# Gate and val of groups 2 to 5 by seven half-size block products instead of eight

## The chip, the cores and the metric

The kernel runs on one core of a Trainium2 chip. The metric is device time in microseconds (us), the median of several runs. In the text PE is TensorE (matmuls; its weight loads are PEld), DVE is VectorE, ACT is ScalarE, POOL is GpSimd, SP is SyncE, which issues most DMAs.

## The reference

Retention attention over 4 batches, 8 heads, 768 positions, 64 channels a head, then RMS norm and a SwiGLU layer over 3072 tokens (512 channels, 1536 hidden):

```python
intra = np.einsum('bhic,bhjc->bhij', qb, kb) * Dmask[None]
intra = np.einsum('bhij,bhjd->bhid', intra, vb)
inter = np.einsum('bhid,bhde->bhie', qb * lam_pow[None], kv_state)
out[:, :, sl] = intra + inter
kv_state = lam_block * kv_state + np.einsum('bhsd,bhse->bhde', kb_dec, vb)
...
xn = x / rms * rms_g
g = xn @ w_gate
silu = g * (1.0 / (1.0 + np.exp(-g)))
val = xn @ w_val
return (silu * val @ w_out).astype(np.float32)
```

All in float32.

## The kernel before, in words

The 3072 tokens make six groups of 512 (m = 0 to 5), the 1536 hidden channels twelve blocks of 128 (f = 0 to 11). A *unit* is one block of one group, written 2.4 for group 2, block 4. The units run in this order: group 0 blocks 0 to 5, all of group 1, group 0 blocks 6 to 11, then groups 2, 3, 4, 5 whole. In the code `u` counts them, so unit 2.0 is u = 24, and the parity of u is that of f there.

To keep float32's precision a matrix is stored as two float16 parts, high and low, and a product is three matmuls: high x high, low x high, high x low. Gate and val of a unit each contract 512 channels in four steps of 128, so each is 12 matmuls of 128x128 weights and 512 tokens into one PSUM bank: gate into `pg`, val into `pv` (function `product`, line 699). Then ACT makes the Silu of `pg` (`sg`, line 784), DVE multiplies with `pv` (`mul`, line 791), ACT casts the high part (`high`, line 801), DVE subtracts the low one (`low`, line 808). One unit later PE multiplies these with `wo`: four out blocks (`out`, t = 0 to 3) of three matmuls each, lines 718 to 720, which add up in four banks `acc` over the twelve units and leave at f = 11.

Between these stands the attention of a later group, one *pair* of heads at a time (class `Pair`): `scores` into `pa` (the two-bank tile of the pool ps_att), `decay_k` (ACT) and `decay_q` (POOL) in place on the loaded `qkv`, `decay_a` (DVE), `state_sums` into `pst`, `states` (DVE), `mix_chunks` and `mix_states` into `po`, then `keep_output` and `keep_squares` (ACT) and `add_squares` (POOL or DVE). `load_next` issues the next DMA.

When a group's four pairs are done, class `Norm` makes its normalized operand: `split_squares` (ACT, POOL), `row_sums` (two matmuls), `seed` and three times `refine` on DVE (each three dependent instructions of 512), then `parts`: for each of four channel blocks `scaled` (DVE), `high` (ACT cast) and `low` (DVE). `halve_o(f)` rewrites `wo` of one block as float16 parts: two instructions on ACT, one on DVE, one add on POOL; the table `HALVE` says in which u.

The order of the work is written by hand: within `tc.manual_schedule` each engine's instructions stand in the order of the code, and the tile framework adds the semaphores. PSUM has eight banks: four `acc`, `pg`, `pv`, and the tile of two in ps_att. Several tags of SBUF buffers are shared: `raw_o` (2 buffers), `in` (4), `w` (1), `t` (3).

Of the kernel before, what the change touches and what calls it, by code (L numbers as in the profile page):

```python
# [9 lines left out]
F32 = mybir.dt.float32  # L10
# [7 lines left out]
P = 128  # L18
# [5 lines left out]
def retention_swiglu_kernel(  # L24
# [146 lines left out]
    WS = 2.0**15  # L171
# [84 lines left out]
    def halve_o(f):  # L256
# [11 lines left out]
        nc.gpsimd.tensor_add(t[:, 1], rest[:, 0], rest[:, 1])  # L268

# [89 lines left out]
    class Weights:  # L359
# [56 lines left out]
        def scale(self, c=slice(0, 2)):  # L416

            if c.start == 0:
# [7 lines left out]
                self.sc[:, c].bitcast(I32), self.e2[:, c], -1.0, float(205 * EXP),  # L426
# [36 lines left out]
    class Pair:  # L463
# [143 lines left out]
    class Norm:  # L607
# [79 lines left out]
        def parts(self):  # L687
            for kk in range(NK):
                self.scaled(kk)
                self.high(kk)  # L690
                if kk:
                    self.low(kk - 1)
            self.low(NK - 1)
# [66 lines left out]

    class Hidden:
# [19 lines left out]

        def silu(self):
            self.sg = tmp.tile([P, G], F32, tag="t", name=f"sg_{self.m}_{self.f}")
            nc.scalar.activation(self.sg, self.pg, AF.Silu, scale=cg[:, self.f, 0:1])  # L784
# [10 lines left out]
        def high(self):  # L795
            if self.half:
                both = hp.tile([P, 2, G], F16, tag="hh", name=f"hh_{self.m}_{self.f}")
# [378 lines left out]
    def unit(u, h, before, late, ready, wt, new, done, norm, step):  # L1176
# [33 lines left out]
        for f in HALVE.get(u, []):  # L1210
            halve_o(f)
        if new and done:
            done.mix()
            done.keep()
# [5 lines left out]
        elif norm:  # L1220
            norm.parts()
# [19 lines left out]
    HALVE = {18: [6, 7], 19: [8, 9], 20: [10, 11], 23: [0, 1], 24: [2, 3], 25: [4, 5]}  # L1241

    with tc.manual_schedule(
# [7 lines left out]
        for u, (m, f) in enumerate(units):  # L1251
# [5 lines left out]
            nxt = max(2, u // NF + 1)  # L1257
            step = u - (nxt * NF - (8 if nxt == 2 else 11))
            new = Pair(nxt, step) if nxt < NG and 0 <= step < NP else None
            done = last if nxt < NG and 1 <= step <= NP else None  # L1260
            if nxt < NG and step == NP + 1:
                norm = Norm(nxt)
                norm.split_squares()
            wt = Weights(TAKE[u]) if u in TAKE else None
            unit(u, h, before, late, ready, wt, new, done, norm, step)
            late, ready = None if wt else ready, wt
            if step == NP + 2:
                norm = None
            before, last = h, new
        before.out()  # L1270
# [72 lines left out]
```

## Time and profile before

| what | value |
|---|---|
| median of 3 runs | 674.52 us (674.17 to 674.59) |
| span of the profiled execution | 673.0 us |
| matmuls on PE | 4143, busy 666.7 us |
| mean granted TensorE clock | 1.000 |
| 128x512 gate matmuls, line 699 | 864 of 379 ns, begun one each 0.216 us |
| the same for val | 864 |
| out matmuls, lines 718 to 720, float16 | 3 x 216 |

In the rows that follow, a group's row reads: line, engine, operation, output<-inputs by the program's names, partitions x elements, count, then busy us and mean ns of one, then the engine's idle time just before these and what ended it. A timeline row reads: start in us, length in us, engine, line, operation, and in brackets the idle time before with its releaser. A row of the waits reads: who waited, for whom, us in all, times, longest. A matmul's own length (379 ns) includes its way through the array; the next begins after 0.216 us.

### The profile page before, as it was taken

Reading aid. Unit: us, or ns where it says so; the run is one execution under the profiler, and the core shown is the slowest. Engines: PE = TensorE matmul, PEld = TensorE weight load, DVE = VectorE, ACT = ScalarE, POOL = GpSimd, SP = SyncE. Lnnn points to the kernel's source line nnn. Section 1 sums busy time; section 2 is a strip of 40 time slices with the busy share of each in tenths; the row PEclk is TensorE's granted clock in tenths of the full one; section 3 lists DMA queues with packets and bytes.
Section 4 is the critical chain, followed back from the end, with each engine's and each line's share of the span. In section 5 each row is a group of like instructions: output and inputs, shape, how many; then the busy total and the mean of one; then the engine's idle time right before and its main releaser. Section 6 shows DMA issues by size and latency. Waiting matters only on the chain.

```text
span 673.0 us, 9893 instructions
## 1 busy us (share of the span) xinstructions
PE 666.7 (99%) x4143; PEld 356.6 (53%) x4143; DVE 322.9 (48%) x575; ACT 248.2 (37%) x438; POOL 78.9 (12%) x76
## 2 busy tenths in 40 slices
PE   9999999999999999999999999999999999999997
PEld 8746665555565444554444555444455444444443
DVE  6798857787464486323712322732332462211112
ACT  3786556676325345222212222221331221211111
POOL 2301030011215203220000111000021000000000
PEclk9999999999999999999999999999999999999999
DMA  8975603441015101131001123000100000100001
GB/s 316 366 245 197 247 7 122 161 156 63 1 64 188 63 0 64 64 126 63 1 0 63 48 79 99 27 0 1 63 1 1 1 0 1 63 0 1 0 1 62
DMA packets 14299, 50.96 MB, mean 76 GB/s; under 512 B 1712, under 2 KB 1968, under 8 KB 12848
## 3 DMA queue, kind: packets, MB, share of 16 engines
q1 hardware_dynamic: 13968, 49.69, 20.5%
q8 instruction: 32, 0.52, 0.3%
q10 hardware_dynamic: 288, 0.66, 0.3%
q14 instruction: 11, 0.09, 0.0%
HBM read 44.05 MB, written 6.29 MB: 75 GB/s over the span
## 4 chain that ended last, share of the span: by engine, by line
PE 97%; DVE 1%; DMA 1%; issue 0%; ACT 0%; DVEq 0%
PE pg L699 28%; PE pv L699 28%; PE acc L718 10%; PE acc L720 9%; PE acc L719 9%; PE pa L478 4%; PE po L538 3%; PE po L549 3%; PE pst L507 2%; PE pss L602 1%; DMA qkv<-in_qkv_dram 1%; DVE xn L677 0%; PE pss L649 0%; DVE w L234 0%; PE unread L146 0%
## 5 line engine op out<-in xcount | busy, mean ns | idle before, releaser
L699 PE MATMUL pg<-x,wg 128*128 128x512 f16 x864 | 200.0, 379 | 0.3 <-ACT x L682 0.3
L699 PE MATMUL pv<-x,wv 128*128 128x512 f16 x864 | 199.0, 379 | 0.0
L791 DVE SCALAR_TENSOR_TENSOR sg<-pv,cv,sg 128x512 f32<-128x512 f32 x54 | 40.5, 750 | 241.7 <-PE pv L699 241.7
L699 PEld LDWEIGHTS <-wv 128*128 128x128 f16 x864 | 83.9, 98 | 101.4 <-issue 1.1
L699 PEld LDWEIGHTS <-wg 128*128 128x128 f16 x864 | 82.5, 98 | 101.4 <-issue 5.0
L720 PE MATMUL acc<-wo,hh 128*128 128x512 f16 (+1 forms) x288 | 110.3, 383 | 0.0
L719 PE MATMUL acc<-wo,hh 128*128 128x512 f16 (+1 forms) x288 | 110.2, 383 | 0.0
L784 ACT ACTIVATE sg<-pg,cg 128x512 f32<-128x512 f32 x72 | 49.3, 685 | 164.7 <-PE pg L699 164.6
L801 ACT CAST hh<-sg 128x512 f16<-128x512 f32 (+1 forms) x72 | 44.5, 618 | 162.0 <-DVE sg L791 158.2
L718 PE MATMUL acc<-wo,hh 128*128 128x512 f16 x216 | 82.0, 380 | 0.0
L498 POOL TENSOR_TENSOR qkv<-qkv,pw 128x512 f32<-128x512 f32 x22 | 28.2, 1284 | 237.6 <-PE pa L478 237.6
L808 DVE TENSOR_TENSOR hh<-sg,hh 128x512 f16<-128x512 f32 x54 | 38.0, 703 | 27.4 <-ACT hh L801 27.4
L718 PEld LDWEIGHTS <-hh 128*128 128x128 f16 x216 | 21.1, 98 | 26.6 <-issue 2.8
L720 PEld LDWEIGHTS <-hh 128*128 128x128 f16 x216 | 21.1, 98 | 25.5
L719 PEld LDWEIGHTS <-hh 128*128 128x128 f16 x216 | 21.2, 98 | 23.4
L494 DVE TENSOR_TENSOR a<-pa,mask 128x1024 f32<-128x1024 f32 x24 | 29.4, 1224 | 6.3 <-PE pa L478 6.2
L718 PE MATMUL acc<-wo,hl 128*128 128x512 f32 x72 | 32.3, 449 | 0.0
L478 PE MATMUL pa<-qkv 64*128 64x128 f32 x384 | 28.8, 291 | 0.1
L478 PEld LDWEIGHTS pa<-qkv 64*128 64x128 f32 x384 | 24.1, 193 | 8.4 <-issue 6.7
L538 PE MATMUL po<-a,qkv 128*64 128x128 f32 x384 | 25.6, 275 | 0.0
L488 ACT ACTIVATE qkv<-qkv,mask 128x256 f32<-128x256 f32 x48 | 21.7, 502 | 8.5 <-DMA qkv<-in_qkv_dram 5.1
L569 ACT COPY x<-po 128x512 f32<-128x512 f32 x22 | 12.8, 581 | 28.6 <-PE po L549 28.6
(131 smaller groups left out, 592.9 us busy)
## 6 DMA issues: line engine op xcount, KB each, us to landing
qkv<-in_qkv_dram SPq DMA_DIRECT2D x47, 512.0 KB, 4.8
raw_gv<-in_weights_dram SPq DMA_DIRECT2D x11, 1024.0 KB, 5.4
raw_o<-in_weights_dram SPq DMA_DIRECT2D x12, 512.0 KB, 3.9
out_dram<-o SPq DMA_DIRECT2D x23, 256.0 KB, 2.3
partial<-in_weights_dram SPq DMA_DIRECT2D x2, 512.0 KB, 12.4
qkv<-in_qkv_dram ACTq DMA_DIRECT2D x1, 512.0 KB, 4.2
out_dram<-o SPq DMA_DIRECT2D x1, 128.0 KB, 2.1
out_dram<-o ACTq DMA_DIRECT2D x1, 128.0 KB, 2.0
```

The source lines that it names most:

```text
L478: nc.tensor.matmul(self.pa[:, j, c, :], self.kT[r, c, :], self.qT[r, c, :], start=True, stop=True,)
L494: nc.vector.tensor_mul(self.a, self.pa, decay.broadcast_to([P, 2, GC, P]))
L498: eng.tensor_mul(self.qT, self.qT, pw[:, p : p + 1, :].broadcast_to([P, GC, P]))
L538: nc.tensor.matmul(po[r, c, :], self.v[:, c, r], self.a[:, j, c, :], start=c == 0, stop=False, skip_group_check=True,)
L699: nc.tensor.matmul(ps, w[:, kk, :], x[:, kk, :], start=i == kk == 0, stop=i == 2 and kk == NK - 1,)
L718: nc.tensor.matmul(acc, hl[:, ts_], oh, start=first, stop=False)
L719: nc.tensor.matmul(acc, hh[:, ts_], ol, start=False, stop=False)
L720: nc.tensor.matmul(acc, hh[:, ts_], oh, start=False, stop=last)
L784: nc.scalar.activation(self.sg, self.pg, AF.Silu, scale=cg[:, self.f, 0:1])
L791: nc.vector.scalar_tensor_tensor(out, self.pv, factor, self.sg, ALU.mult, ALU.mult)
L801: nc.scalar.copy(self.hh, self.sg)
L808: nc.vector.tensor_sub(self.hl, self.sg, hh)
```

## The change

For groups 2 to 5 gate and val are computed together as a product of 2x2 blocks: rows val and gate, inner index the two channel halves of 256, columns the two token halves of 256 (`HG`). Strassen's scheme in Winograd's form takes seven block products. A product is 6 matmuls of 128x128 weights and 256 tokens (three part products, two channel steps). The unit has 42 matmuls of 256 columns in place of 24 of 512.

- `weight_sums(f)` makes four sums of the weight blocks, once for each f: POOL adds high and low into `r` (two adds of 512), DVE makes four sums of 256, ACT casts the high parts (512, 256, 256), POOL subtracts the low parts. For f = 0 to 5 it follows units 0.6 to 0.11; for f = 6 to 11 (`LATE`) units 2.2 to 2.7. In `HALVE` blocks 0 to 5 are halved in units 0.9 to 0.11, formerly in 0.11 to 2.1.
- `Norm.parts` is made in two calls, and makes three sums of operand blocks more in each (`sums` on DVE, `high_sums` on ACT, `low_sums` on POOL, 768 wide). They lie in two tiles `tx`, which take two of the four `in` buffers; so `load_next` skips two calls for group 2.
- A unit (`unit_of_sums`) has two banks a and b: in even units `pg` and `pv`, in odd units the two halves of the ps_att tile (`pp`). The products go in the order 1 (a), 2 (b), 6 (a), 5 (b, anew), 7 (a), 4 (a), 3 (b). ACT copies a away after products 1, 6 and 7 (`keep`); DVE adds bank b to such a copy (`sum`) after products 2, 7 and 3. Silu is made in two halves, `mul_sums` reads SBUF alone.
- The out blocks come two units later instead of one. Pairs of the next group stand in units f = 0 to 7, one pair per two units: scores in the even, states and mixing in the odd. The norm stands in f = 8 (row sums, seed, one refinement), 9 (two refinements), 10 and 11 (parts).
- The weights' exponent constants change with the head room that the sums need.

```diff
-    WS = 2.0**15
+    WS = 2.0**13
...
-            load_next()
+            if self.m > 2 or self.p < 2:
+                load_next()
...
+        def sums(self, i):
+            a, b = self.xns[i], self.xns[2 + i]
+            a1, a2, b1, b2 = a[:, :HG], a[:, HG:], b[:, :HG], b[:, HG:]
+            t = stage.tile([P, 3, HG], F32, tag="raw_o", name=f"xt_{self.m}_{i}", bufs=2)
+            self.xt = t
+            nc.vector.tensor_sub(t[:, 0], a2, a1)
+            nc.vector.tensor_sub(t[:, 2], b2, a2)
+            nc.vector.tensor_sub(t[:, 1], b2, t[:, 0])
+            nc.vector.tensor_sub(a2, b1, t[:, 1])
+        def high_sums(self, i):
+            nc.scalar.copy(tx[SLOT_OF[self.m]][:, 0, i], self.xt)
+        def low_sums(self, i, eng=nc.gpsimd):
+            t = tx[SLOT_OF[self.m]]
+            eng.tensor_sub(t[:, 1, i], self.xt, t[:, 0, i])
+        def parts(self, i, engs):
+            self.scaled(i)
+            self.scaled(2 + i)
+            self.sums(i)
+            self.high(i)
+            self.high(2 + i)
+            self.high_sums(i)
+            self.low(i, engs[0])
+            self.low(2 + i, engs[1])
+            self.low_sums(i, engs[2])
...
+    def weight_sums(f, rest):
+        r = cvt.tile([P, 2, G], F32, tag="w", name=f"r_{f}")
+        for i, w in enumerate((wv, wg)):
+            nc.gpsimd.tensor_add(r[:, i], w[:, f, 0], w[:, f, 1])
+        v0, v1, g0, g1 = (r[:, i, j * HG : (j + 1) * HG] for i in range(2) for j in range(2))
+        t = stage.tile([P, 4, HG], F32, tag="raw_o", name=f"ws_{f}", bufs=2)
+        nc.vector.tensor_add(t[:, 0], g0, g1)
+        nc.vector.tensor_sub(t[:, 2], v0, g0)
+        nc.vector.tensor_sub(t[:, 1], g1, t[:, 2])
+        nc.vector.tensor_sub(t[:, 3], v1, t[:, 1])
...
+        nc.scalar.copy(s12[:, 0], t[:, :2])
+        nc.scalar.copy(s3[:, 0], t[:, 2])
+        nc.scalar.copy(s4[:, 0], t[:, 3])
+        nc.gpsimd.tensor_sub(s12[:, 1], t[:, :2], s12[:, 0])
+        nc.gpsimd.tensor_sub(s3[:, 1], t[:, 2], s3[:, 0])
+        nc.gpsimd.tensor_sub(s4[:, 1], t[:, 3], s4[:, 0])
...
+        def add(self, n, ps, first):
+            w, x = self.pairs[n - 1]
+            for i, (ow, ox) in enumerate(((0, 0), (1, 0), (0, 1))):
+                for k in range(2):
+                    nc.tensor.matmul(
+                        ps, w(ow, k), x(ox, k), start=first and i == k == 0,
+                        stop=i == 2 and k == 1, skip_group_check=True,
+                    )
...
+        def banks(self, u):
+            m, f = self.m, self.f
+            if u % 2:
+                t = ps_att.tile([P, 2, G], F32, tag="ps", name=f"pp_{m}_{f}")
+                self.pa, self.pb = t[:, 0, :HG], t[:, 1, :HG]
+            else:
+                self.pa = ps_gv.tile([P, G], F32, tag="pg", name=f"pa_{m}_{f}")[:, :HG]
+                self.pb = ps_gv.tile([P, G], F32, tag="pv", name=f"pb_{m}_{f}")[:, :HG]
...
+        def keep(self, i):
+            nc.scalar.copy(self.kept[:, i], self.pa)
+        def sum(self, out, i):
+            nc.vector.tensor_add(out, self.pb, self.kept[:, i])
...
-    HALVE = {18: [6, 7], 19: [8, 9], 20: [10, 11], 23: [0, 1], 24: [2, 3], 25: [4, 5]}
+    HALVE = {18: [6, 7], 19: [8, 9], 20: [10, 11], 21: [0, 1], 22: [2, 3], 23: [4, 5]}
+    def unit_of_sums(u, h, prev, outs, new, done, norm, step):
...
+        h.add(1, a, True)
+        h.add(2, b, True)
+        h.keep(0)
+        if prev:
+            prev.high()
+        h.sum(h.val[:, left], 0)
+        if prev:
+            prev.low()
...
+        if norm and step == 10:
+            norm.parts(0, (nc.gpsimd, nc.gpsimd, nc.gpsimd))
+        if norm and step == 11:
+            norm.parts(1, (nc.vector, nc.vector, nc.gpsimd))
+        h.add(4, a)
+        h.silu_half(0, a)
...
+        h.add(3, b)
+        h.sum(h.val[:, right], 1)
+        h.mul_sums()
+        if u in LATE:
+            weight_sums(LATE[u], None)
+    LATE = {26 + i: HALF + i for i in range(HALF)}
```

What that does to the order of instructions shows at three places. The first is ACT from unit 0.10 to unit 0.11. Before, between the two Silus (`sg`) stand the cast of the hidden part `hh` and the four casts of the norm (`x`):

```order
L784 ACTIVATE sg_10_2417<-pg_10_2404,cg 128x512
L801 CAST hh_10_2433<-sg_10_2417 128x512
L682 CAST x_1992<-xn_0_2436 128x512
L682 CAST x_1992<-xn_1_2439 128x512
L682 CAST x_1992<-xn_2_2443 128x512
L682 CAST x_1992<-xn_3_2447 128x512
L784 ACTIVATE sg_11_2477<-pg_11_2464,cg 128x512
```

The same place on ACT after the change; `wo` and `rest` are the halving, `tx` the sums of operand blocks, and the casts from `ws` those of the weight sums:

```order
L933 CAST hh_10_2497<-sg_10_2481 128x512
L263 ACTIVATE wo_2_2500<-wo_755,ts 128x512
L264 ACTIVATE rest_2501<-wo_755,ts 128x512
L263 ACTIVATE wo_3_2506<-wo_885,ts 128x512
L264 ACTIVATE rest_2507<-wo_885,ts 128x512
L684 CAST x_1992<-xn_0_2512 128x512
L684 CAST x_1992<-xn_2_2514 128x512
L701 CAST tx_2467<-xt_0_2516 128x768
L815 CAST wo_10_2318<-ws_2542 128x512
L816 CAST col<-ws_2542 128x256
L817 CAST wg<-ws_2542 128x256
L915 ACTIVATE sg_11_2566<-pg_11_2553,cg 128x512
```

Four halving instructions and four casts of sums have come ahead of the Silu of unit 0.11, each of which needs DVE or POOL first.

The second place is ACT from the last units of a group into the next group. Before, at the step from group 4 to group 5, only Silu, cast and, for two instructions, the output stand there (`o`):

```order
L784 ACTIVATE sg_11_4810<-pg_11_4797,cg 128x512
L801 CAST hh_11_4826<-sg_11_4810 128x512
L784 ACTIVATE sg_0_4854<-pg_0_4841,cg 128x512
L801 CAST hh_0_4870<-sg_0_4854 128x512
L727 ACTIVATE o_1_4882<-acc_0_1_4198,ik 128x512
```

After the change, from unit 3.11 into unit 4.0; the copies to `tx` are `keep`, and `sg` from a `pp` or `pa` bank is the half of Silu that reads PSUM:

```order
L897 COPY tx_2467<-pp_11_4779 128x256
L933 CAST hh_10_4794<-sg_10_4697 128x512
L897 COPY tx_2467<-pp_11_4779 128x256 x2
L904 ACTIVATE sg_11_4780<-sg_11_4780,cg 128x256
L684 CAST x_3952<-xn_1_4832 128x512
L684 CAST x_3952<-xn_3_4834 128x512
L701 CAST tx_2467<-xt_1_4836 128x768
L904 ACTIVATE sg_11_4780<-pp_11_4779,cg 128x256
L897 COPY tx_2466<-pa_0_4862 128x256
L933 CAST hh_11_4878<-sg_11_4780 128x512
```

The second part of the norm's casts has moved to unit 11, between the two halves of a Silu.

The third place is PE in a unit of group 5, with the engine whose semaphore an instruction waits for in brackets. Before, in unit 5.6, PE waits for the banks once each:

```order
L699 LDWEIGHTS wg
L699 MATMUL pg_6_5121<-x_4283,wg 128x512 [waits Activation_49]
...
L699 LDWEIGHTS wv
L699 MATMUL pv_6_5136<-x_4283,wv 128x512 [waits DVE_49]
...
L718 LDWEIGHTS hh_5_5106 [waits DVE_49]
L718 MATMUL acc_0_0_4929<-wo_5_2653,hh_5_5106 128x512
L719 LDWEIGHTS hh_5_5106 [waits Activation_49]
```

After, in the odd unit 5.3; the products that begin with a wait are 6 (`wo_9`, which holds sums 1 and 2), 5, 4 and 3 (`wg`):

```order
L743 MATMUL acc_0_0_6104<-wo_1_2418,hh_1_6100 128x512
L854 LDWEIGHTS wo_9_2229
L854 MATMUL pp_3_6157<-tx_2466,wo_9_2229 128x256 [waits DVE_49]
...
L854 MATMUL pp_3_6157<-tx_2466,wo_9_2229 128x256 [waits Activation_49]
...
L743 MATMUL acc_0_3_6138<-wo_1_2418,hh_1_6100 128x512
L854 LDWEIGHTS wg
L854 MATMUL pp_3_6157<-x_5025,wg 128x256 [waits DVE_49]
...
L854 MATMUL pp_3_6157<-x_5025,wg 128x256 [waits Activation_49]
```

Where the bank was given back once a unit, it is now given back four times, and in odd units products 6 and 4 wait for DVE, products 5 and 3 for ACT.

More of the change, by code (lines that the diff above doesn't have):

```diff
@@ L759, in finish, with operand_tiles @@
             out_product(m, f, hh, hl, t, first, last, m == 0, half)
+    HG = G // 2
+    tx = []
+    pairs12 = []
+    third = []
+    def operand_tiles():
+        for i in range(2):
+            t = stage.tile([P, 4, 2, HG], F32, tag="in", name=f"tx_{i}", bufs=4)
+            both = t.bitcast(F16).rearrange("p a b (c g) -> p (a b c) g", c=2)
+            tx.append(both[:, :12].rearrange("p (o i j) g -> p o i j g", o=2, i=2))
+            rest = t.rearrange("p a b g -> p (a b) g")[:, 6:]
+            copies.append(rest)
@@ L1211, in unit @@
             halve_o(f)
+        if u == FACTORS:
+            squares = col.bitcast(F16).rearrange("p a f c -> p (a f c)")
+            squares = squares.rearrange("p (f o g) -> p f o g", f=HALF, o=2)
+            third.extend(squares[:, f] for f in range(HALF))
         if new and done:
```

161 lines of the change are left out of this document (141 added, 20 removed).

## The prediction

> **What bounds the kernel now.** I read the page's busy times first, then the chain of work that ended last, then the waits.
>
> ```profile
> span 673.0 us, 9893 instructions
> PE 666.7 (99%) x4143; PEld 356.6 (53%) x4143; DVE 322.9 (48%) x575; ACT 248.2 (37%) x438; POOL 78.9 (12%) x76
> PE 97%; DVE 1%; DMA 1%; issue 0%; ACT 0%; DVEq 0%
> DVE sg L791 <- PE pv L699: 246.8, 52, 7.6
> ACT sg L784 <- PE pg L699: 164.6, 54, 5.3
> ```
>
> TensorE (PE) carries 97% of the chain, and ACT and DVE wait for it. Fewer streamed columns on PE therefore shorten the run one for one, as long as nothing makes PE wait. How it now avoids waiting shows in unit 0.10 (group 0, block 10; rows of the chain, then ACT's instructions in order of time):
>
> ```profile
> 241.68 2.59 PE pg L699 x12
> 244.27 2.59 PE pv L699 x12
> 246.86 0.22 PE acc L718
> 246.84 0.62 ACT L682 CAST x<-xn 128x512 f16<-128x512 f32 x1 [0.70 <-DVE xn L677]
> 247.36 0.68 ACT L784 ACTIVATE sg<-pg,cg 128x512 f32<-128x512 f32 x1
> ```
>
> The gate ended at 244.27, but its Silu started at 247.36: it stands in ACT's queue behind four casts of the norm, which wait for DVE. Engines work in the order written. These 3.1 us cost nothing, because PE needs the bank `pg` back only after val (2.59) and the out block (12 x 0.216). That cover is what the change removes: it needs a bank back after 0.65 to 2 us.
>
> **What a matmul of 256 columns takes.** Twelve matmuls of 512 columns take 2.59 us: 0.2158 each, loads hidden. Beside them stand one-column matmuls, each with a weight load of its own:
>
> ```profile
> 180.30 0.17 PE L306 MATMUL pc<-ones_b,col 128*128 128x1 bf16 x1
> 180.32 0.38 PE L699 MATMUL pg<-x,wg 128*128 128x512 f16 x1
> 180.54 0.16 PE L306 MATMUL pc<-ones_b,col 128*128 128x1 bf16 x1
> ```
>
> One of each takes 0.24, so one column costs 0.024, load included. At 256 columns the bounds are half of 0.2158 (0.1079) and the straight line between the two forms (0.120). A load is ready after some 0.024, far less than the stream, so I take 0.109, near the lower end. Before: 48 units x 24 x 0.2158 = 248.6 us. After: 48 x 42 x 0.109 = 219.7 (217.5 to 241.9). **Term 1: -28.9 us** (-31.1 to -6.7), the whole possible gain.
>
> **Durations for the added work.**
>
> ```profile
> L729 DVE TENSOR_SCALAR o<-acc,ik 128x256 f32<-128x256 f32 x1 | 0.5, 475 | 0.0
> L727 ACT ACTIVATE o<-acc,ik 128x256 f32<-128x256 f32 x1 | 0.5, 474 | 1.1 <-DVE o L729 1.1
> L685 DVE TENSOR_TENSOR x<-xn,x 128x512 f16<-128x512 f32 x20 | 13.6, 687 | 0.6
> L677 DVE SCALAR_TENSOR_TENSOR xn<-x,gs,hy 128x512 f32<-128x512 f32 x16 | 11.6, 745 | 0.0
> L682 ACT CAST x<-xn 128x512 f16<-128x512 f32 x24 | 14.7, 616 | 13.1 <-DVE xn L677 12.9
> L784 ACT ACTIVATE sg<-pg,cg 128x512 f32<-128x512 f32 x72 | 49.3, 685 | 164.7 <-PE pg L699 164.6
> L791 DVE SCALAR_TENSOR_TENSOR sg<-pv,cv,sg 128x512 f32<-128x512 f32 x54 | 40.5, 750 | 241.7 <-PE pv L699 241.7
> L263 ACT ACTIVATE wo<-wo,ts 128x512 f16<-128x512 f32 x12 | 8.6, 720 | 6.7 <-DVE rest L265 6.7
> L268 POOL TENSOR_TENSOR wo<-rest 128x512 f16<-128x512 f32 x12 | 15.3, 1273 | 41.1 <-DVE rest L265 40.4 <-ACT sg L784 0.7
> L685 POOL TENSOR_TENSOR x<-xn,x 128x512 f16<-128x512 f32 x4 | 4.6, 1166 | 7.6 <-ACT x L682 7.6
> L274 POOL TENSOR_TENSOR col<-sq_w 128x256 bf16<-128x256 bf16 x12 | 8.4, 708 | 74.5 <-DVE sq_w L273 74.5
> 230.95 0.75 DVE L791 SCALAR_TENSOR_TENSOR sg<-pv,cv,sg 128x512 f32<-128x512 f32 x1 [3.11 <-PE pv L699]
> 231.74 0.62 ACT L801 CAST hh<-sg 128x512 f16<-128x512 f32 x1 [2.66 <-DVE sg L791]
> 233.00 0.68 DVE L656 TENSOR_SCALAR hy<-pss 128x512 f32<-128x512 f32 x1
> 236.42 0.69 DVE L667 TENSOR_TENSOR yt<-hy 128x512 f32<-128x512 f32 x1
> 238.60 0.69 DVE L667 TENSOR_TENSOR yt<-hy 128x512 f32<-128x512 f32 x1
> 249.40 0.72 ACT L263 ACTIVATE wo<-wo,ts 128x512 f16<-128x512 f32 x1
> 250.03 0.70 ACT L264 ACTIVATE rest<-wo,ts 128x512 f32<-128x512 f32 x1
> 477.74 1.16 PE L478 MATMUL pa<-qkv 64*128 64x128 f32 x16
> 478.83 0.57 PE L507 MATMUL pst<-qkv 128*64 128x64 f32 x12
> ```
>
> From these: a hop between engines 0.04 (231.70 to 231.74); an independent instruction begins 0.09 before the last ends (249.40, 250.03); seed with one refinement 3.42 (233.00 to 236.42), a refinement 2.18; scores 1.09. Not in the trace, bounded by the nearest form and half or twice of it: DVE 256 wide, SBUF to SBUF, 0.34 to 0.475: 0.42, so four 1.68; `keep` and casts of 256 on ACT 0.31 to 0.474: 0.40; a cast of 768 0.62 to 1.23: 0.80; POOL adds of f16 `r` 1.17 to 1.27: 1.2; POOL of 768 1.27 to 2.3: 1.7.
>
> **A plain unit** becomes 7 products x 0.654 + 12 x 0.216 = 7.17 us on PE, against 7.77. In even units each wait is covered: product 6 needs `keep` of bank a (0.65 + 0.4 + hops, before 1.96). In odd units both banks are one tile, and PE waits for the tile's last reader. Product 6 then waits for `keep` and the DVE sum after product 2: 0.4 + 0.475 + 3 hops = 1.0, against 0.65 of cover: 0.35. Product 3 waits for the Silu of product 4, written just ahead of it: 0.474 + 2 hops = 0.55. With pair work the state sums and two out blocks cover both; group 5 has none. **Term 2: 6 odd units x 0.9 = +5.4 us** (0 to 8).
>
> **Before each next group** (three times; units f = 8 to 11 of groups 2 to 4):
> - f = 9, product 6: after the row sums DVE does seed and refinement 3.42, two sums 0.95, mul 0.69, hops 0.16 = 5.2; PE has four products and an out block, 3.3. Wait 1.9.
> - f = 9, product 4: `low` 0.69, two refinements 4.35, sum and hops 0.58 = 5.6 against three products and three out blocks, 3.9. Wait 1.7. Product 3: 0.55.
> - f = 11, product 6, counted from product 7 of f = 10: keep and sum 0.95, two `scaled` 1.49, four sums 1.68, three casts 2.04, Silu 0.474, mul 0.69, sum 0.475, hops 0.24, less 0.5 of overlaps = 7.5; PE has 4.5 of work. Wait 3.0. The Silu stands behind the casts, as at 247.36 above; `keep` behind it.
> - f = 11, product 3: 0.95 + 1.49 + 1.68 + 2.04 - 0.4 + 0.474 + 0.12 = 6.35 against 1.95. Wait 4.4.
>
> Together 11.5; **term 3: x 3 = +34.6 us** (24 to 42). The four-cast norm of before was hidden, so nothing comes off.
>
> **Weight sums in units 2.2 to 2.7**: ACT's casts stand ahead of the next unit's first `keep`.
> - Next unit odd (three): DVE sum 0.475, mul 0.69, four sums 1.68, casts 1.42, keep 0.4, sum 0.475, hops 0.28, less 0.5 = 4.9; PE has 2.5. Wait 2.4.
> - Next unit even: from product 4, Silu 0.474, square 0.6, POOL's adds 1.27 + 2.4, sums 1.68, casts 1.42, keep 0.4, less overlaps = 7.9, against 4.4. Wait 3.5, twice; 2.1 the third time, where DVE adds the squares.
> - Unit 2.1 has no out block to cover it: 1.3.
>
> **Term 4: +17.6 us** (9 to 24).
>
> **Weight sums and halvings in units 0.6 to 0.11.** Here Silu of the next unit waits behind everything of this one:
> - 0.10: Silu 0.69, mul 0.75, high 0.62, halving: ACT 0.72, DVE 0.75, POOL 1.27, DVE 0.75, POOL 1.27 (one shared buffer is left, so in turn); norm sums 1.68, casts 2.04, POOL 1.7, adds 2.4, sums 1.68, casts 1.42, hops less overlaps -0.2 = 17.5, against PE's 7.77. Wait 9.8.
> - 0.11 to product 6 of 2.0: the same round from the Silu's end, with `keep`: 17.3 against 1.31 + 1.09. Wait 14.9.
> - 0.9: Silu to high 2.06, halving 0.72 + 0.75 + 2.54, three refinements with seed 7.7, sums 1.68, casts 1.42, less overlaps = 16.2, against 8.2. Wait 8.0.
> - 0.6 to 0.8: rounds of some 14 against 11.3 with pair work; `decay_k` stands behind the casts: 5 (0 to 8).
>
> **Term 5: +37.7 us** (28 to 42).
>
> At no cost: the second shift of the out blocks (the last unit's tail is hidden by one of them as before); the exponent constants; loads of qkv with two buffers less, since a load lands in 4.8 us and two units stand between (gone, 4.8 per pair).
>
> ```profile
> qkv<-in_qkv_dram SPq DMA_DIRECT2D x47, 512.0 KB, 4.8
> 4.95 2.06 PE L478 MATMUL pa<-qkv 64*128 64x128 f32 x16
> 12.38 1.16 PE L478 MATMUL pa<-qkv 64*128 64x128 f32 x16
> ```
>
> The last two rows are the same work early and later: 0.9 more in the first 8 us. The trace has no long idle stretch of PE afterwards, so it does not tell whether the slow phase would return. I put it at 0. It can be up to some 2.5 (three such blocks) for each of seven long waits, 17.
> The Trainium skill's page "TensorE: Matmul & The Clock Gate" (What's actually happening) says that PE falls to half its clock after about 3.4 us of idling and needs as long of work to recover. By it the seven waits over 4 us could each add up to 1.7, an estimate of 12 at most; without it the sum stays.
>
> **Sum:** -28.9 + 5.4 + 34.6 + 17.6 + 37.7 = +66.4. The profiled execution spans 673.0, the median of the runs is 674.52; the 1.5 between stays. 674.5 + 66.4 = **740.9 us**.
>
> **Rivals.**
> - *The clock falls during the long waits* (last rows above). For it, the slow start; against it, that much of PE's slow work would lie inside the chains of the other engines. 740.9 + 4 to 17: about 750.
> - *The weight load limits at 256 columns*, 0.120 each: +22, 763. For it, twice as many loads per column; against it, 0.024 for load and column.
> - *The other side: the helpers run ahead.* DVE is 48%, ACT 37%, POOL 12% busy; if their work for norm and weights slips into idle stretches early enough that `keep` is never late, term 1 stands alone: 645.6. It decides where the waits, 95.3 us by my terms, come to less than 28.9, 30% of that. Against it, the Silu at 247.36: queues do not let a ready instruction pass.
>
> **Numbers.** Forecast 0.70, clock 0.13, load 0.10, helpers ahead 0.07 (0.05 faster, 0.01 same, 0.01 slower). 0.2% is about what this measurement can tell from no change. So faster 0.05, same 0.01, slower 0.94. Range: waits a fifth smaller, 722; the load case, 764.
>
> **What would show it.** Matmuls of 256 columns 0.109 apart; PE's share under 92% for the first time; in the waits, PE waiting for ACT's `tx` copies and for DVE's sums, longest (over 8 us) where group 2 begins; ACT's longest waits before the casts of `ws` and `tx`, for DVE and POOL. I am wrong if POOL's adds are done before ACT reaches the casts, or if PE's idle time in groups 3 and 4 is near 0.

## The result, and the profile after

The changed kernel takes 771.46 us (median of 4 runs, 768.7 to 773.1) against 674.56 us for the kernel before on the same chip: a ratio of 1.143 (95% interval 1.140 to 1.146). The prediction said slower, 740.9 us with a range of 722 to 764. The direction was right; the time lies 7 us above the range. The profiled execution took 771.88 us and spans 769.9, which is 96.9 more than the 673.0 before.

From the page of the changed kernel: the span, the engines' busy times, PE in 40 slices with the clock granted to it, and the chain by engine.

```profile
span 769.9 us, 12275 instructions
PE 675.0 (88%) x5007; PEld 450.4 (58%) x5007; DVE 420.5 (55%) x793; ACT 329.9 (43%) x674; POOL 161.0 (21%) x150
PE   9999999999987718887977799997899997799997
PEclk9999999999988957989999999998899999899999
PE 69%; DVE 16%; ACT 8%; POOL 4%; issue 2%; DMA 1%; DVEq 0%; SPq 0%; ACTq 0%; POOLq 0%
```

PE has fallen from 99% of the span to 88%: it now idles for some 95 us, and DVE, ACT and POOL carry 28% of the chain. One thing surprises. PE's busy time went up, from 666.7 to 675.0, though it streams fewer columns. Most of the reason stands in the last row but one: the granted clock is below full speed in slices from about 250 us on, at the dips of the row of PE. The rest is that the matmul ahead of each wait is recorded a little past the end of its stream (0.17 us, see below).

What PE waited for, longest sums first:

```profile
PE pp L854 <- DVE vals L900: 21.5, 16, 3.0
PE pp L854 <- ACT sg L904: 17.8, 13, 4.2
PE pa L854 <- ACT tx L897: 12.4, 4, 3.5
PE pa L854 <- ACT sg L915: 9.9, 1, 9.9
PE pa L854 <- ACT x L684: 9.2, 1, 9.2
PE pst L508 <- ACT sg L915: 4.9, 1, 4.9
PE pp L854 <- DVE sg L900: 4.8, 4, 1.5
```

`pp` is the tile of two banks of the odd units; L900 is DVE's sum, L904 the Silu half, L897 `keep`. The three longest single waits lie where group 2 begins or ahead of it, in group 0. ACT's instructions there, in order of time, and PE's first two of unit 2.0:

```profile
268.56 1.14 ACT L684 CAST x<-xn 128x512 f16<-128x512 f32 x2 [3.87 <-DVE xn L698]
269.61 0.83 ACT L701 CAST tx<-xt 128x768 f16<-128x768 f32 x1
275.65 0.62 ACT L815 CAST wo<-ws 128x512 f16<-128x512 f32 x1 [5.21 <-DVE ws L810]
276.17 0.40 ACT L816 CAST col<-ws 128x256 f16<-128x256 f32 x1
276.48 0.40 ACT L817 CAST wg<-ws 128x256 f16<-128x256 f32 x1
276.78 0.68 ACT L915 ACTIVATE sg<-pg,cg 128x512 f32<-128x512 f32 x1
277.51 0.37 PE L854 MATMUL pa<-x,wv 128*128 128x256 f16 x1 [9.93 <-ACT sg L915]
287.06 1.22 PE L854 MATMUL pa<-x,wv 128*128 128x256 f16 x5 [9.18 <-ACT x L684]
```

The Silu of unit 0.11 stands behind the norm's casts and the casts of `ws`, and these behind DVE and POOL. PE idles 9.93 us for the bank, and 9.18 more for the second half of the norm. By stretch (span in us, then the busy times of PE, its weight loads, DVE, ACT and POOL, the granted clock, DMA): first the kernel before from 0.7 to 2.1, then the changed kernel from 0.7 to 2.1, from 2.1 to 3.0, and group 3.

```profile
204.20:257.10 52.90, 52.90 (x312) 26.01 (x312) 30.87 (x46) 23.69 (x41) 13.88 (x11) 1.00 0.19 70
```

```profile
203.60:303.00 99.40, 64.10 (x345) 33.48 (x345) 54.19 (x86) 37.85 (x72) 52.95 (x48) 0.79 0.06 22
303.00:430.80 127.80, 101.32 (x810) 70.48 (x809) 65.34 (x125) 46.05 (x105) 44.82 (x40) 0.93 0.11 38
430.80:548.00 117.20, 106.60 (x877) 75.49 (x875) 56.44 (x104) 44.39 (x97) 14.50 (x12) 0.96 0.14 46
```

No engine is full in any of them: from 0.7 to 2.1 DVE and POOL, the busiest helpers, work 54 and 53 of 99 us. So no engine lacks time for the work as such; whether its order loses the time is for the experiments below. And every one of these stretches has a granted clock under 1, where the kernel before has 1.00.

### The profile page after: what moved, and what is told of

Its sections match the earlier page's. It is cut to its first block, busy times and chain, and to the rows that moved or that the text cites. A ratio compares the mean times of both kernels' runs of the same rounds, so it can differ in the third digit from the quotient of the medians.

```text
span 769.9 us, 12275 instructions
## 1 busy us (share of the span) xinstructions
PE 675.0 (88%) x5007; PEld 450.4 (58%) x5007; DVE 420.5 (55%) x793; ACT 329.9 (43%) x674; POOL 161.0 (21%) x150
## 3 DMA queue, kind: packets, MB, share of 16 engines
q1 hardware_dynamic: 13968, 49.69, 18.2%
## 4 chain that ended last, share of the span: by engine, by line
PE 69%; DVE 16%; ACT 8%; POOL 4%; issue 2%; DMA 1%; DVEq 0%; SPq 0%; ACTq 0%; POOLq 0%
PE pp L854 13%; PE pa L854 8%; PE acc L741 7%; PE pg L722 6%; PE pv L722 6%; PE acc L743 6%; PE acc L742 6%; PE pb L854 6%; PE pa L479 3%; PE po L539 3%; POOL r L805 2%; PE po L550 2%; DVE xn L679 1%; DVE sg L909 1%; DVE yt L670 1%
## 5 line engine op out<-in xcount | busy, mean ns | idle before, releaser
L854 PEld LDWEIGHTS <-wo 128*128 128x128 f16 x576 | 57.7, 103 | 66.3 <-issue 44.7
L722 PE MATMUL pg<-x,wg 128*128 128x512 f16 x288 | 67.8, 380 | 3.3 <-ACT sg L915 3.0
L897 ACT COPY tx<-pp 128x256 f32<-128x256 f32 x72 | 26.7, 371 | 102.5 <-PE pp L854 102.5
L722 PE MATMUL pv<-x,wv 128*128 128x512 f16 x288 | 66.8, 379 | 0.0
L897 ACT COPY tx<-pa 128x256 f32<-128x256 f32 x72 | 26.8, 372 | 87.9 <-PE pa L854 87.6
L854 PE MATMUL pp<-tx,wo 128*128 128x256 f16 x288 | 42.5, 287 | 21.5 <-DVE vals L900 21.5
L854 PE MATMUL pp<-x,wg 128*128 128x256 f16 x288 | 40.5, 278 | 22.6 <-ACT sg L904 17.8
L900 DVE TENSOR_TENSOR vals<-pp,tx 128x256 f32<-128x256 f32 x48 | 20.3, 424 | 61.2 <-PE pp L854 50.1
L940 DVE TENSOR_TENSOR hh<-sg,hh 128x512 f16<-128x512 f32 x54 | 41.5, 768 | 11.1 <-ACT hh L933 8.7
L900 DVE TENSOR_TENSOR vals<-pb,tx 128x256 f32<-128x256 f32 x48 | 20.3, 424 | 46.7 <-PE pb L854 38.4
L909 DVE SCALAR_TENSOR_TENSOR sg<-vals,cv,sg 128x512 f32<-128x512 f32 x48 | 39.0, 812 | 9.0 <-ACT sg L904 5.9
L854 PE MATMUL pa<-x,wv 128*128 128x256 f16 x144 | 21.8, 290 | 19.1 <-ACT sg L915 9.9
L743 PEld LDWEIGHTS <-hh 128*128 128x128 f16 x216 | 21.8, 101 | 27.7 <-issue 3.8
```

The costliest lines, as they stand in the source:

```text
L722: nc.tensor.matmul(ps, w[:, kk, :], x[:, kk, :], start=i == kk == 0, stop=i == 2 and kk == NK - 1,)
L743: nc.tensor.matmul(acc, hh[:, ts_], oh, start=False, stop=last)
L854: nc.tensor.matmul(ps, w(ow, k), x(ox, k), start=first and i == k == 0, stop=i == 2 and k == 1, skip_group_check=True,)
L897: nc.scalar.copy(self.kept[:, i], self.pa)
L900: nc.vector.tensor_add(out, self.pb, self.kept[:, i])
L909: nc.vector.scalar_tensor_tensor(self.sg, self.val, cv[:, self.f : self.f + 1], self.sg, ALU.mult, ALU.mult)
```

## The experiments

**Pauses alone.** The first question is what lowers the clock. The kernel before, with pauses put into it and no seven-product work:

```diff
+    def gap(columns):            # between gate and val of 24 units of groups 2 to 5
+        nc.tensor.matmul(ps[:, 0, :P], ident, ident, start=True, stop=True)
+        nc.vector.tensor_mul(junk[:, :P], ps[:, 0, :P], ident)
...                               # as many DVE multiplications as `columns` says
+        nc.vector.tensor_mul(junk[:, :P], junk[:, G : G + P], ident)
+        nc.tensor.matmul(ps[:, 1, :P], junk[:, :P], ident, start=True, stop=True)
```

> The kernel before, unchanged in its result, with 24 pauses of PE between gate and val in units of groups 2 to 5: PE waits for a chain of DVE multiplications on data that nothing else reads, of 640 to 3072 columns, single pauses of some 1 to 4.5 us and six pairs of short ones with four matmuls between. No seven-product work is in it. Theory A (the clock is set window by window on a grid of 3.413 us: after a window in which PE idles more than about 2 us, in one piece or in two, the next window runs at half clock and takes up to 1.7 us more for its work): pairs of 1.1 to 1.5 us can start a spell, single pauses of 2.0 to 2.8 do so only where they fall into one window, longer ones always. Theory B (a single idle stretch of 2 us or more starts it, wherever it lies): no pair does, every single pause over 2 us does. Theory C (about 3.4 us of idling are needed, as the Trainium skill's page "TensorE: Matmul & The Clock Gate" has it): only the pauses over 3.4 us. Time: 674 plus some 55 to 65 us of pauses plus 1.7 for each spell.

It took 815.5 us (one run). Two of its pauses, PE in order of time, and then four windows of 3.4 us on the grid around them (PE's busy time is the second number, the granted clock the third from the end):

```profile
664.42 0.38 PE L1186 MATMUL gap_ps<-ident 128*128 128x128 f32 x2
667.30 0.49 PE L1193 MATMUL gap_ps<-ident,gap_a 128*128 128x128 f32 x2 [2.50 <-DVE gap_a L1192]
667.62 4.44 PE L699 MATMUL pv<-x,wv 128*128 128x512 f16 x12
703.73 0.38 PE L1186 MATMUL gap_ps<-ident 128*128 128x128 f32 x2
707.33 0.49 PE L1193 MATMUL gap_ps<-ident,gap_a 128*128 128x128 f32 x2 [3.22 <-DVE gap_a L1192]
707.66 2.75 PE L699 MATMUL pv<-x,wv 128*128 128x512 f16 x12
```

```profile
664.60:668.00 3.40, 0.90 (x6) 0.52 (x6) 2.30 (x5) 0.69 (x1) 0.00 (x0) 1.00 0.39 148
668.00:671.40 3.40, 3.40 (x10) 1.22 (x8) 0.00 (x0) 0.00 (x0) 0.00 (x0) 0.51 0.00 0
702.20:705.60 3.40, 1.91 (x10) 0.96 (x8) 1.41 (x3) 0.69 (x1) 0.00 (x0) 1.00 0.00 0
705.60:709.00 3.40, 1.67 (x9) 0.95 (x10) 1.58 (x4) 0.00 (x0) 0.00 (x0) 1.00 0.00 0
```

The shorter pause, 2.50, lies in one window: PE is busy 0.90 of 3.40, the next window has the clock 0.51, and the twelve matmuls of val take 4.44 in place of 2.75. The longer pause, 3.22, is cut by a border: 1.91 and 1.67 busy, no window falls, val takes 2.75. All 15 slow spells of the run begin on one grid of 3.413 us. Of the 37 windows at full speed with over 0.9 us idle, all 15 with 1.97 or more were followed by a slow one, and none of the 22 with 1.94 or less. A slow window (one at half clock) was followed by another where PE idled 0.82 or more in it (5 times), and by full speed at 0.57 or less (15 times). So B and C fall: a pause of 2.50 was enough, one of 3.22 was not. Of theory A the windows hold; its "longer ones always" does not, as the 3.22 shows, and whether two pieces count together this run does not tell, since no two pauses in one window came to more than 1.84. (The pairs are seven, not six.) The time was over the estimate because the pauses were longer than planned: the waits add up to 90 us, not 55 to 65; the slow windows add 27, the rest is the pause's own matmuls.

**Filled waits.** The same cause in the changed kernel, from the other side:

```diff
+    def fill(n):                 # ahead of 15 waiting instructions
+        for _ in range(n):
+            nc.tensor.matmul(accs[0], zero16, wv[:, 0, 0], start=False, stop=False, ...)
```

> At 29 of the places where PE was seen to wait in the changed kernel, matmuls with a weight tile of zeros are written ahead of the waiting instruction (8 to 86 of 512 columns, 0.216 us each, a little less than the wait seen there), accumulating zeros into an out bank; the rest is the changed kernel. Theory A (PE's idle stretches of 2 us and more start the half-speed spells, and these cost the 23 us by which the matmuls in them last longer): the granted clock goes from 0.949 to about 1.00, idle time of PE nearly vanishes, and the time falls by about 23 us, from 771 to 748 (745 to 753). Theory B (the spells come from something else, or lie inside the chains of the other engines and cost nothing): time 771 or more, since the fillers shorten no wait.

(The places are 15; the 29 is a miscount.) 758.54 us, ratio to the kernel before 1.123 (1.118 to 1.127). The clock came to 0.993, the slow windows from 79 us to 10, and the time fell by 12.9 us: theory B is out, but A's 23 was too much, and the time lies over its range. Where the other half stayed is seen stretch by stretch. From unit 2.1 to the end the slow matmuls of the changed kernel last 15.7 us longer than at full speed; fill leaves 4.9 of that, and the stretch is 11.1 shorter, the whole of what was taken away. From 0.7 to 2.1 the excess is 7.6, all gone in fill, and the stretch is 2.1 shorter: there the chain of ACT, DVE and POOL sets the end, and a slow matmul lies inside a wait that gets longer without it.

The three spells that are left, one at f = 9 of each group, show what the pauses could not. Two of them have 1.54 and 0.56 us of idling in one window, 2.1 together, and the third 1.54 and 0.36. PE around the second, products 4 and 3 of unit 3.9 and the next unit's products 1 and 2, which run at half speed:

```profile
515.52 0.81 PE L868 MATMUL pp<-x,wg 128*128 128x256 f16 x6 [1.54 <-DVE sg L914]
516.89 1.00 PE L868 MATMUL pp<-x,wg 128*128 128x256 f16 x6 [0.56 <-ACT sg L918]
517.68 1.49 PE L868 MATMUL pa<-x,wv 128*128 128x256 f16 x6
518.97 1.49 PE L868 MATMUL pb<-x,wv 128*128 128x256 f16 x6
```

**The sums of weights.**

```diff
     def weight_sums(f, rest):
+        return
```

> The sums of the weights (POOL, DVE and ACT work after the last product of each unit) are left out, and products 5 to 7 read raw weights in their place, so the output is not the reference's; PE does the same number of matmuls. Theory A (in groups 0 to 2 the waits come from the sums of weights): units 2.2 to 2.7 lose their 17 us of waits, the stretch from 0.7 to 2.0 loses about 22 us (halvings and the norm stay), with some 10 us of half-speed spells: about 722 (712 to 732). Theory B (the halvings, now three units earlier and over the norm, and the norm of two halves cause the waits there, and the sums lie beside them): only the 17 us and their spells, 3 to 6 us, go: about 750.

718.75 us, ratio 1.066 (1.065 to 1.068): 52.7 less than the changed kernel, theory A (712 to 732). From 0.7 to 2.1 it takes 70.5 us in place of 99.4, and the waits of units 2.2 to 2.8 are gone. What is left against 52.9 before must lie with the halvings and the norm in two halves, the other work added there; no run separates them.

**Is it the sums, or where they stand?**

```diff
+        if u in LATE: weight_sums(LATE[u], 0)     # POOL's adds: at the unit's start
...
         h.silu_half(1, h.sg[:, right])
+        if u in LATE: weight_sums(LATE[u], 1)     # DVE's four sums
...
         h.silu_half(0, a)
+        if u in LATE: weight_sums(LATE[u], 2)     # ACT's casts, POOL's subtractions
...
-        if u in LATE: weight_sums(LATE[u], None)  # all of it, at the unit's end
```

> In units 2.2 to 2.7 the sums of weights are written in three places in place of one: POOL's first two adds at the unit's start, DVE's four sums after the first Silu half, ACT's three casts and POOL's three subtractions after the second Silu half; the same instructions in all. Theory A (the waits of 1.8 to 3.5 us there come from ACT's casts, which stand in its queue ahead of the next unit's keep while they wait for POOL and DVE): most of these 15 us go, with spells of about 7: 771 - 20 = 751 (748 to 757). Theory B (the work itself is too much for the time of a unit, wherever it is written): the waits move to products 4 and 3 of the same unit, 765 to 775.

751.31 us, ratio 1.114 (1.111 to 1.116): 20.2 less, on theory A's number. PE's waits for `keep` (`pa <- ACT tx`) fall from 12.4 us in four to 3.5 in one, the one at the start of group 2. The same for the first six blocks, from the ends of 0.6 to 0.11 to the starts and middles of later units:

```diff
-            if FACTORS <= u < FACTORS + HALF:
-                weight_sums(u - FACTORS, None)
+    SUMS = {19: 0, 20: 1, 22: 2, 23: 3}           # unit number: block, in unit()
+    LATE = {24: 4, 25: 5} | {26 + i: HALF + i for i in range(HALF)}
```

> As the kernel with spread sums in units 2.2 to 2.7 (751.3), and the sums of weights 0 to 5 as well taken from the ends of units 0.6 to 0.11: POOL's first adds at the start of units 0.7, 0.8, 0.10, 0.11, 2.0 and 2.1, DVE's sums ahead of the multiplication and ACT's casts right behind the Silu (in 2.0 and 2.1 as in 2.2). Theory A (here too it is the place: Silu of the next unit stands behind the casts of this one): without these sums the stretch from 0.7 to 2.1 took 70.5 us against 99.4; with them out of the way it takes 72 to 85, so 751 - 14 to 27: about 731. Theory B (POOL is the limit there: 53 of the 99 us, with the halvings in turn through one buffer): the stretch stays over 92 us, 745 to 753.

737.79 us, ratio 1.095 (1.090 to 1.100): 13.5 less again, just short of theory A's 14 to 27. The stretch from 0.7 to 2.1 came to 87.4, not 72 to 85: one wait of 15.3 is left at the first product of 2.0, for the norm's casts. They still stand behind halvings in ACT's queue, and also behind the casts of the sum of block 3, which belong to unit 0.11 and wait 4.63 us for DVE, which itself waits 3.89 for POOL's adds. PE's wait, then ACT's:

```profile
PE pa L865 <- ACT x L684: 15.3, 1, 15.3
272.67 0.62 ACT L825 CAST wo<-ws 128x512 f16<-128x512 f32 x1 [4.63 <-DVE ws L817]
```

So these sums found a better place, but not a free one: with them the kernel is still 19.0 us over the one without sums.

**The norm in other places.**

```diff
-        if norm and step == 9: norm.refine(); norm.refine()   # ahead of product 7
+        if norm and step == 9: norm.refine()      # one behind low, one behind the Silu half,
...                                                # one behind the last product; f = 8 keeps the seed
-            norm.parts(1, (nc.vector, nc.vector, nc.gpsimd))
+            norm.parts(1, None)                   # f = 11: scaled and sums alone
         h.add(4, a)
         h.silu_half(0, a)
+        if norm and step == 11: norm.casts(1, (nc.vector, nc.vector, nc.gpsimd))
```

> The changed kernel with the norm of the next group written in other places of units f = 8 to 11 in groups 2 to 4, the same instructions in all: of the three refinements one stands behind the low part of f = 9, one behind its first Silu half, one behind its last product; in f = 11 the three casts and the subtractions after them stand behind the second Silu half. Theory A (these waits are places in the queues of ACT and DVE): the waits of f = 9 (1.7 and 1.5) vanish, those of f = 11 (3.0 and 3.8 to 4.2) shrink to some 2.6 in all, since product 1 of the next group then waits for the subtractions: 3 x (3.2 + 4.5) = 23 us less, with a spell or two of half speed per group: 746 (740 to 751). Theory B (DVE's chain of refinements and sums sets the time, wherever it stands): the waits move to products 1, 5 and 6 behind it and the time stays within 5 us of 771.

753.25 us, ratio 1.117 (1.114 to 1.121): 18.2 less, 2 us over A's range and far outside B's. Of the waits of f = 9 the 1.5 is gone and the 1.7 became 0.3, the 0.56 at product 3 stayed, and the 4.2 of f = 11 became 1.0 at the next group's start. The 3.0 at product 6 of f = 11 stayed: it comes from the first half's casts in f = 10, which this edit leaves in place. I had counted it as movable.

**Two banks or one tile.**

```diff
-                t = ps_att.tile([P, 2, G], F32, tag="ps", name=f"pp_{m}_{f}")
+                self.pa, self.pb = (two[0].tile([P, G], F32, tag=f"p{i}", ...)[:, :HG] for i in range(2))
```

> In group 5 the odd units take two separate one-bank tiles in place of the two banks of one tile; nothing else. Theory A (PE waits for the last reader of the whole tile): the odd units fall from 8.33 to the 7.17 of the even ones, 6 x 1.16 = 7.0 us less, 764.5 (763 to 766). Theory B (the odd units wait for ACT and DVE as such, since keep and Silu are late): no change, 771.

765.24 us, ratio 1.134 (1.132 to 1.137): 6.2 less, theory A. An odd unit of group 5, PE in order of time: products 6, 5, 7 and 3 in the changed kernel, then product 6 with this edit:

```profile
707.78 0.81 PE L854 MATMUL pp<-tx,wo 128*128 128x256 f16 x6 [0.27 <-DVE vals L900]
709.08 0.82 PE L854 MATMUL pp<-tx,wo 128*128 128x256 f16 x6
709.73 0.82 PE L854 MATMUL pp<-tx,col 128*128 128x256 f16 x6
713.06 0.81 PE L854 MATMUL pp<-x,wg 128*128 128x256 f16 x6 [0.56 <-ACT sg L904]
```

```profile
702.76 0.82 PE L856 MATMUL p<-tx,wo 128*128 128x256 f16 x6
```

In the last row the wait is gone with nothing changed on DVE: product 6 needs bank a, and DVE was reading bank b.

**All four moves together.**

> The four moves together: sums spread in both places, norm in other places, two banks in group 5; the same work as the changed kernel. Theory A (the four are independent, all of them queue places): 771 - 20 - 20 - 6 - 25 = 700 (690 to 712). Theory B (they share one cover, so that a wait taken away at one place comes back at the next): over 720. In either case above 674, since the stretch where group 2 begins keeps 20 us or more of waits.

715.85 us, ratio 1.061 (1.059 to 1.063), 55.6 less than the changed kernel. That is over A's 690 to 712 and under B's 720. The single edits measured 33.7 (both sums), 18.2 (norm) and 6.2 (banks), 58.1 in all, so they are nearly independent, as A says; its sizes were too large, by the two misses above. 18 us of waits for `x` are left, 15.4 of them where group 2 begins.

**Seven products where there is cover.** Group 5 has no next group to prepare, and group 4's units of eight products leave ACT and DVE time. The loop of the kernel before runs to the end of group 4:

```diff
-        for u, (m, f) in enumerate(units[: 2 * NF]):
+        for u, (m, f) in enumerate(units[: 5 * NF]):
+    SUMS = {4 * NF + f + 1: f for f in range(5)} | {4 * NF + 4 + f: f for f in (5, 6, 7)}
+    LATE = {5 * NF + i: 8 + i for i in range(4)}
```

> Seven products in group 5 alone: groups 0 to 4 run the loop of the kernel before, with its halvings and its norm of four casts (the norm of group 5 in two halves, with the sums of tokens); one sum of weights per unit in eight units of group 4 (behind the gate of its own block) and in the first four of group 5, spread; group 5 with two one-bank tiles in odd units. Theory A (the gain of 0.60 us per unit is real where the long cover of the units before hides the preparation): 12 x 0.60 = 7.2 us less than the kernel before, at most 2 of it lost where group 5 begins: 668 (666 to 671). Theory B (the sums of weights and the half norm make the gates of group 4 wait as they did in group 0): 676 or more.

679.15 us, ratio 1.006 (1.004 to 1.007): 0.6% slower, theory B. PE's waits in it, the one for `unread` at the start left out:

```profile
PE pg L731 <- DVE state L525: 2.6, 1, 2.6
PE p L874 <- ACT tx L922: 1.8, 3, 1.1
PE pv L731 <- DVE sg L947: 1.5, 1, 1.5
```

Each is again an instruction that PE needs, standing behind a sum in a queue: DVE's `states`, ACT's `keep`, DVE's multiplication. So those sums were moved, and then one more:

```diff
-    SUMS = {4 * NF + f + 1: f for f in range(5)} | {4 * NF + 4 + f: f for f in (5, 6, 7)}
-    LATE = {5 * NF + i: 8 + i for i in range(4)}
+    SUMS = {4 * NF + f: f for f in range(HALF)} | {4 * NF + 4 + f: f for f in (6, 7)}
+    LATE = {5 * NF + 2 + 2 * i: 8 + i for i in range(4)}
```

> As the kernel with seven products in group 5 alone (679.2), with the sums of weights in other places, after what its trace showed: its gate of block 2 in group 4 waited 2.6 for DVE's states behind the first sums, val of block 10 waited 1.5 for a multiplication behind late sums, and product 6 in group 5 1.1 twice for a keep behind casts. Now six sums stand at the ends of units 4.0 to 4.5 (POOL's adds at their starts), two before the multiplication of 4.10 and 4.11, four in units 5.2, 5.4, 5.6 and 5.8. Theory A (those waits were queue places and no more): 7.2 us of gain less 0.5 to 1.5 at the seam: 668 (667 to 671), faster than before. Theory B (the preparation does not fit beside group 4 and 5, wherever it stands): 674 to 680.

672.74 us, ratio 0.997 (0.996 to 0.998): 0.3% faster than the kernel before and clear of B, but 1.7 over A's range. One wait was new, 2.0 us of the row sums for POOL, with a slow window behind it:

```profile
PE pss L652 <- POOL sr L646: 2.0, 1, 2.0
```

```diff
-    SUMS = {4 * NF + f: f for f in range(HALF)} | {4 * NF + 4 + f: f for f in (6, 7)}
-    LATE = {5 * NF + 2 + 2 * i: 8 + i for i in range(4)}
+    SUMS = {4 * NF + f: f for f in range(5)} | {4 * NF + 4 + f: f for f in (6, 7)}
+    LATE = {5 * NF + 2 + 2 * i: f for i, f in enumerate((5, 8, 9, 10, 11))}
```

> As the kernel with seven products in group 5 alone whose sums were moved (672.7), with one sum of weights moved again: that of block 5, from the end of unit 4.5 to unit 5.2; those of blocks 8 to 11 go to 5.4, 5.6, 5.8 and 5.10. In the trace of that kernel unit 4.5 takes 12.17 us against 8.27 in the kernel before: its row sums wait 2.0 for POOL's part of the squares, which stands behind the subtractions of that sum, and a half-speed spell follows (1.7). Theory A: those 3.9 us go and little comes in group 5 (even units have 0.4 us of slack for keep): 672.7 - 3.5 = 669 (668.3 to 670.2). Theory B (the sum costs as much in group 5, where nothing covers it): 671.5 to 673.

669.70 us, ratio 0.993 (0.991 to 0.994), theory A. It beats both kernels, the one before by 0.7%. Its page and its longest wait behind the start:

```profile
span 669.0 us, 10621 instructions
PE 661.1 (99%) x4359; PEld 378.4 (57%) x4359; DVE 370.1 (55%) x667; ACT 278.7 (42%) x524; POOL 144.5 (22%) x138
```

```profile
PE pg L731 <- DVE state L525: 0.5, 1, 0.5
```

5.0 of the 7.2 us that seven products save in group 5 arrive: group 5 takes 94.2 us against 99.9, and unit 4.1 is 0.7 longer. The rest is small waits such as the last row's. (The unit of 12.17 us in this expectation is 4.6; the sum in its way stood at the end of 4.5.)

## Why the prediction was wrong

By its own steps, against the rows of the changed kernel:

| step | predicted, us | measured, us | from |
|---|---|---|---|
| term 1, streaming | -28.9 | -28.9 by the rate, some -25 over all | 0.65 from 709.08 to 709.73 for six, 0.109 each; the rest below |
| term 2, odd units of group 5 | +5.4 | 7.0 | 8.33 - 7.17 a unit, six times; 6.2 by the banks |
| term 3, before each next group | +34.6 | 32.5 | waits in f = 9 and 11 of three groups |
| term 4, sums in 2.2 to 2.7 | +17.6 | 15.3 | 1.81 three times, 3.49 twice, 2.01; 0.30 and 0.57 in 2.1 |
| term 5, sums and halvings in 0.6 to 0.11 | +37.7 | 35.3 | 9.93, 9.18, 3.45, 4.90, 2.74, 2.08, 3.02 |
| clock after the waits | 0 | 23.3 | excess of the matmuls in 79 us of half clock |

The waits of term 3, those of group 2 as an example, came where the prediction put them (1.9 and 1.7 at products 6 and 4 of f = 9; 3.0 and 4.4 in f = 11); the first of them is not shown here:

```profile
404.87 0.82 PE L854 MATMUL pp<-x,wg 128*128 128x256 f16 x6 [1.54 <-DVE sg L900]
419.21 1.44 PE L854 MATMUL pp<-tx,wo 128*128 128x256 f16 x6 [3.02 <-DVE vals L900]
429.60 1.44 PE L854 MATMUL pp<-x,wg 128*128 128x256 f16 x6 [4.16 <-ACT sg L904]
```

All waits together are 90.1 by these rows. The recorded end of a matmul lies 0.17 behind the end of its stream (0.82 for six against 0.65 from start to start), so each of the 30 waits of terms 3 to 5 is that much longer, some 5 in all (term 2's 7.0 has it in): about 95, against 95.3 predicted, and with these ends each of the four terms is within 2 us. Terms 2 to 5 held, and the runs with moved sums and a moved norm show that the cause was the one named: instructions that stand in a queue ahead of the one PE waits for. The run with two tiles shows term 2's: a bank that waits for the other bank's reader.

The step that failed is the last one before the sum: "The trace has no long idle stretch of PE afterwards, so it does not tell whether the slow phase would return. I put it at 0." It returned 12 times and the matmuls in it took 23.3 us longer. That is the greater part of the 30.5 us by which the forecast change, +66.4, fell short of 96.9. In the last three rows it shows as 1.44 in place of 0.82 for the six matmuls behind a wait of 3.02 or 4.16, while behind 1.54 it is 0.82. The rival that had this mechanism was mis-sized too. It gave 4 to 17 from seven waits over 4 us, or 12 by the Trainium skill's page "TensorE: Matmul & The Clock Gate" (What's actually happening), read there as 3.4 us of idling. That page of the Trainium skill says that the window is free-running and 3413 ns long, which the grid of the pauses agrees with; the measured condition is weaker than an idle window, some 1.95 us of idling in one. Nine of the twelve spells follow waits of terms 3 and 4, the two of f = 11 in each group and the three over 2 us in units 2.4 to 2.8; the other three follow term 5's waits of 4.90, 2.74 and 9.93. What speaks for weighing this rival higher stood in the prediction's own rows: 2.06 and 1.16 for the same sixteen matmuls.

Not all of the 23.3 is a cost by itself, as the filled waits showed: 13 of it came off when PE was kept at work. With -28.9, the 95 and the 23.3 the sum is 89 of the 96.9. Of the 7 us left some 4 belong to term 1, which took the 0.60 of a plain unit for every unit. Units 3.0 to 3.7, which hold the attention of the next group, take 73.7 us against 76.4 before, and 4.0 to 4.7 take 75.4 against 77.3. Without the slow matmuls at their start (0.85 and 1.6) each eight save 3.5 and not 4.8, though PE has no recorded wait there; 1.3 a group, if group 2 does as these two. Why is open, and some 3 us I cannot place.

The other rivals: a limit by weight loads at 256 columns did not show (0.109, not 0.120), and the helpers did not run ahead. A slip to correct: the rows from 241.68 to 247.36 in the prediction belong to unit 0.11, not 0.10. The casts stand between `high` of 0.10 and the Silu of 0.11, and the argument is the same.

## What to carry to other kernels

Fewer columns on a full TensorE are worth their time only where every hand-back of a bank still fits under its cover; when a change divides a long use of a bank into short ones, write down each instruction ahead of the one that gives the bank back, on its engine, and add up. Preparation then costs more by its place than by its amount: the same sums cost 52.7 us at the ends of the units and 19.0 when the early part was issued at a unit's start and the casts behind the instruction that PE needs. Take a saving first where nothing has to be prepared beside it (the last group here, -0.7%), and count a wait of about 2 us or more on TensorE as dearer than it looks, since what follows it may run at half speed.

## What was not expected of the hardware

- The granted clock goes down by windows of 3.413 us on a grid of its own. In the run with pauses it fell after 1.97 us of idling in one window and not after 1.94; in a slow window 0.82 idle kept it slow and 0.57 did not. Two pieces count together, as the filled waits show (1.54 and 0.56). In the traces of the other kernels the border is less sharp: windows with 1.81, 1.82 and 1.91 idle were followed by slow ones (two tiles, filled waits), and some with 1.98 to 2.01 were not (no sums, moved sums, two tiles); of the slow windows one with 0.72 idle stayed slow and one with 0.79 did not. At full speed 1.95 idle leaves 1.45 us of work in the window, at half speed 1.3 to 1.4 us worth, so it may be the work done that counts; this is an estimate that no run here tests. The grid has no tie to the program: the changed kernel and the one with two tiles are the same up to group 5, yet in their profiled runs unit 2.7 takes 11.91 and 13.53 us, and unit 2.8 11.50 and 9.81. The times of the changed kernel scatter over 4.4 us, those of the kernel before over 0.7 beside it and up to 2.6 in other rounds; I take the grid for part of the cause, though no run isolates it.
- DVE's instructions that read two operands of 512 columns from SBUF last longer where POOL is at work. The multiplication of the halves in units 2.1 to 2.11 (POOL busy 44.8 of 127.8 us), and in group 5, where POOL rests:

```profile
L909 DVE SCALAR_TENSOR_TENSOR sg<-vals,cv,sg 128x512 f32<-128x512 f32 x11 | 10.2, 928 | 2.7 <-ACT sg L904 2.0
L909 DVE SCALAR_TENSOR_TENSOR sg<-vals,cv,sg 128x512 f32<-128x512 f32 x10 | 7.5, 751 | 0.7
```

  One by one it is plainer: in the changed kernel the 43 multiplications with POOL idle last 751 ns at the mean and 753 at most, the 5 that POOL's work covers 1331. The sums of 256 columns that read a bank kept their 424 ns. The Trainium skill's "GPSIMD Engine Reference" (Key points) says that the two engines share their ways into SBUF and hinder each other with two SBUF inputs; the rows agree, and no run here takes POOL's work away by itself. The prediction had 0.69 for this instruction everywhere.
